# A second tile for the natural layout of x, and an earlier load of the third block, in a convolution and feed-forward kernel

## The chip, the cores and the metric

The kernel runs on one core of a Trainium2 chip. The metric is the device time of that core in microseconds, lower being better. The engines are named as the profile names them: PE for the matrix engine (PEld for its weight loads), DVE for the vector engine, ACT for the scalar engine, POOL for the general purpose engine, and SP for the engine that only issues transfers. "SPq" and "POOLq" in a profile line stand for the queue of such an engine. Each engine takes its instructions in the order in which they were put into its queue, and waits at an instruction until the semaphores that it names have been counted up.

## The reference

```python
x:      (8, 4096, 192) float32      weight: (8, 7) float32
w_in:   (192, 2048) float32         w_out:  (2048, 192) float32

w = softmax(weight, axis=-1)                       # 8 heads of 24 channels, 7 taps
y[b, s, c] = sum_k w[head(c), k] * x[b, s - 6 + k, c]   # causal, zeros before s = 0
x2 = y.reshape(32768, 192)
h  = x2 @ w_in
out = (h * sigmoid(h)) @ w_out                     # (32768, 192) float32
```

A short causal convolution over the sequence, with one set of seven taps for each head, is followed by a feed-forward layer with a SiLU.

## The kernel before

The 32768 tokens are worked through in 32 blocks of 1024 tokens (two halves of 512). A block passes through these stages, each with its function:

- `load` (line 132): twelve transfers on SP, issued on line 140, of 64 KB each, bring the block's x into the tile `nat`. There is one such tile. It has 128 partitions (32 tokens or channels for each of four groups) and three slices, one for each `k`, so four transfers belong to each slice.
- `turn_in` (line 422): DVE transposes one slice of `nat` into `xt` (line 425), so that channels lie on the partitions.
- `halo_in` (line 437): the six columns of `xt` ahead of each half are filled. For the first half POOL copies them from a small tile `tail` (line 442), which was saved from the block before. For the second half SP issues a transfer from the end of the first half (line 443). Then the end of this block is saved for the next (`tail_of`, line 435, a transfer on SP).
- `conv` (line 446): seven taps for each slice. From the third block on, the first tap is a multiplication on DVE (line 454) and the other six are multiply-adds on DVE (line 457). They read `xt` with its six extra columns and write their result back into `nat`, over the x that was there.
- `spread` (line 464): SP copies a finished slice of `nat` into the tile `dup` (line 474), in an arrangement that PE can use.
- `win` (line 478): DVE forms sums and differences of `dup` (lines 491 and 494).
- `product` and `plain` (lines 579 and 591): the first matrix product on PE. ACT copies partial results out of PSUM (line 615), DVE adds them up (line 611, `X`, `a` and `b` in the plan), and ACT applies the SiLU (lines 627 and 632).
- `sum_g` and `out_slot` (lines 635 and 653): differences of the results on DVE, and the second matrix product on PE (line 683).
- `merge`, `turn_out`, `store_out`: the results are combined on DVE and ACT, transposed on DVE (line 764) and stored by SP (line 772).

Both products use a scheme with fewer multiplications than a plain one, which needs sums and differences of the weights. Blocks 1 to 31 take this form. While the first block runs in a plain form (`up_plain`, `down_plain`, lines 529 and 702), DVE converts the float64 weights (`round_in`, `round_out`, all recorded on line 123) and POOL forms the sums of weights (`combine` and `combine_out`, recorded on line 319). A few 192 KB transfers that POOL issues itself (line 307, `ws<-wr`) supply POOL with swapped halves of the weights.

The order of the work is written out by hand in the string `PLAN`. Its slots are separated by bars, and each holds tokens: `i.1` is `turn_in` of slice 1 of the next block, `ha.0` its `halo_in`, `v.10` tap 0 of slice 1 of the next block's convolution, `sp.2` its `spread` of slice 2, `ld.1` a load of slice 1, `X2.0` one of the additions on line 611. A leading `-` means the block before, and `+` the block after. The plan is run once per block, for block numbers 1 to 33, after a separate piece of code for the first block. `step` leaves out whatever is in the set `did`. Instructions made by the wrappers `vec`, `act`, `pool` or `pin` keep the order in which the program gives them. The others, among them the transfers of `load` for any block but the first, are placed by a scheduler.

Because `nat` holds x first and the convolution's result later, the x of the next block can be loaded into a slice only when `spread` has copied that slice's result away. In the plan, `ld.0` comes at the end of a block (`+ld.0`) and `ld.1` and `ld.2` near the start of the next.

Around the end of the first block the program gives, in this order: the convolution of the second block, which is still going on beside `down_plain`, its three spreads, its `win` steps, three transposes and twelve stores of the first block's output, `+ld.0` for the third block, and then the plan for block 1, in which the DVE runs `i.1`, `i.2`, `i.0`, then `v.10`, `v.00`, `v.01`, `v.02`, `v.11`, `v.12` for the third block, and then `X2.0`.

Of the kernel before, what the change touches and what calls it, by code (L numbers as in the profile page):

```python
# [9 lines left out]
F32 = mybir.dt.float32  # L10
# [7 lines left out]
def kernel(  # L18
# [31 lines left out]
    P = 128  # L50
    R = 64
    NK = D // R
    grp = D // H
    pad = K - 1
    TB = 512
# [5 lines left out]
    SQ = 32  # L61
# [8 lines left out]
    xpool = ctx.enter_context(tc.tile_pool(name="xp", bufs=1))  # L70
# [44 lines left out]
    def pin(ins):  # L115
        return tc.keep_in_program_order(ins)
# [13 lines left out]
    nats, xts, gs = {}, {}, {}  # L130

    def load(b, ks=range(NK)):
        if b not in nats:
            nats[b] = nats[0] if b else xpool.tile([P, NK, TB // SQ, SQ], F32, tag="nat", name="nat")
        nat = nats[b]
        for k in ks:
            for i in range(P // SQ):
                c = R * k + SQ * (i % 2)
                queue = nc.scalar if not b and k == 0 and i % 2 == 0 else nc.sync
                ins = queue.dma_start(  # L140
                    out=nat[SQ * i : SQ * i + SQ, k, :, :],
                    in_=x_v[2 * b + i // 2][:, :, c : c + SQ],
                )
                if not b:
                    pin(ins)
# [32 lines left out]
    for k in range(NK):  # L178
        rows_k = hot[SQ * k : SQ * k + SQ]
        for sign, base in ((1, 0), (-1, grp - 1)):  # L180
# [5 lines left out]
                base=base + sign * R * k,  # L186
# [4 lines left out]
    for e in range(2):  # L191
# [6 lines left out]
            base=0,  # L198
# [166 lines left out]
    def combine_out(j):  # L365


        def a_(u, a):
            return wo[j][:, a, :, HD * u : HD * u + HD]

        x_ = [wx[j][:, i, :, :] for i in range(3)]
        comb(x_[0], a_(1, 0), a_(1, 1), ALU.add)
        comb(x_[1], x_[0], a_(0, 0), ALU.subtract)
        comb(x_[2], a_(0, 1), x_[1], ALU.subtract)
        comb(a_(1, 0), a_(0, 0), a_(1, 0), ALU.subtract)
# [191 lines left out]
    def product(b, g, r):  # L567
        e = int(r in ON_B and (g, r) != SWAP)
        if r in RIGHT:
            rhs = rows(wins[b], e)[:, RIGHT[r], :]  # L570
        else:
            rhs = rows(dups[b], e)[:, SLOT[e][X_OF[r]], :]
        if r in (13, 11):
            to, first = banks[XBANK[2 if r == 13 else 4]], False
        else:
            c = next(c for c in range(3) if r in CHAINS[c])
            to, first = chain_bank(g, c), r == CHAINS[c][0]
        pin(
            nc.tensor.matmul(  # L579
                to, raw(g, *LEFT[e][r], e), rhs, start=first, stop=True, skip_group_check=True  # L580
            )
        )

    def plain(b, n, k):
        a, j, own = PLAIN
        first = (b, n) not in begun
        begun.add((b, n))
        for e in range(2) if n else (0,):
            cols = slice(e * TB // 2, (e + 1) * TB // 2) if n else slice(0, TB)
            pin(  # L590
                nc.tensor.matmul(  # L591
                    banks[PLAIN_BANKS[n and 1 + e]][:, cols],
                    rows(wr[j] if own == e else ws[j], e)[:, a, k, :],
                    rows(dups[b], e)[:, SLOT[e][2 * k + n], cols],
                    start=first,
                    stop=True,
                    skip_group_check=True,
                )
            )
# [5 lines left out]
    def sums_h(b, name, g):  # L605

        o = int(name[1:])
        t1, t2, t3 = (chain_bank(g, c) for c in range(3))

        def add(out_, u, v, op=ALU.add):  # L610
            pin(nc.vector.tensor_tensor(out_, u, v, op=op))  # L611

        if name[0] == "u":
            us[b, g, o] = upool.tile([P, TB], F32, tag="u", name="u")
            pin(nc.scalar.copy(us[b, g, o], t1))  # L615
        elif name[0] == "X":
            add(banks[XBANK[o]], us.pop((b, g, o)), t2)
        elif name[0] == "a":
            add(h_of(b, g, o), us.pop((b, g, o)), t2)
        elif name[0] == "b":  # L620
            c = us.get((b, g, o), None)
            c = h_of(b, g, o) if c is None else c
            add(c, c, t3, ALU.subtract)
        else:
            h = h_of(b, g, o)
            src = {3: t1, 2: banks[XBANK[2]], 4: banks[XBANK[4]]}.get(o, h)
            pin(nc.scalar.activation(h, src, AF.Silu))  # L627

    def silu_plain(b, i):
        cols = slice((i - 1) * TB // 2, i * TB // 2) if i else slice(0, TB)  # L630
        h = h_of(b, None, int(i > 0))[:, cols]
        pin(nc.scalar.activation(h, banks[PLAIN_BANKS[i]][:, cols], AF.Silu))


    def sum_g(b, j, i):

        t = sums.setdefault((b, j), {})
        if i // 2 not in t:
            t[i // 2] = tpool.tile([P, 2, 2 * TB], F32, tag="t", name="t")

        def of(a, n):
            return gs[b, j, a][:, n, :, :].rearrange("p e t -> p (e t)")

        u, v = (
            (lambda: (of(0, 1), of(0, 0))),
            (lambda: (of(1, 1), t[0][:, 0, :])),
            (lambda: (of(1, 1), of(0, 1))),
            (lambda: (of(1, 0), t[0][:, 1, :])),
        )[i]()
        engine = pool if f"t.{j}{i}" in ON_POOL else vec  # L650
        engine.tensor_tensor(t[i // 2][:, i % 2, :], u, v, op=ALU.subtract)
# [106 lines left out]
    def turn_out(b, i):  # L758
        if b not in osbs:
            osbs[b] = tpool.tile([P, 4, TB // SQ, SQ], F32, tag="t", name="osb")  # L760
        osb = osbs[b]
        top = HD if b else P
        pin(
            nc.vector.transpose(
                osb[0:top, i, :, :].rearrange("p k c -> p (k c)"), cmbs[b][0][0:top, i, :]
            )
        )

    def store_out(b, i):
        for q in range((HD if b else P) // SQ):  # L770
            n, c = (i % 2, HD * (i // 2) + SQ * q) if b else (q // 2, R * i + SQ * (q % 2))
            nc.sync.dma_start(  # L772
                out=out_v[2 * b + n][:, :, c : c + SQ], in_=osbs[b][SQ * q : SQ * q + SQ, i, :, :]
            )

    plan = [slot.split() for slot in PLAN.split("|")]
    did, later = set(), []
    closing = f"S3.{QUEUE[-1]}"
    BACK = {"-": 1, "=": 2, "+": -1}
    base = {t.lstrip("-=+") for s in plan for t in s}  # L780
# [9 lines left out]
    def step(b, token):  # L790

        if token[0] in BACK:
            b, token = b - BACK[token[0]], token[1:]
        name, arg = token.split(".") if "." in token else ("", "")
        if b < 0 or b >= NB or not name or (b, token) in did:
            return
        if b == NB - 1 and token in held:
            return
        if b == NB - 1 and token[:3] == "D3." and (b, closing) not in did:
            later.append(token)  # L800
            return
        did.add((b, token))
        digits = [int(c) for c in arg]
        if name[0] == "P":
            product(b, digits[0], int(name[1:]))
        elif name == "L":
            plain(b, *digits)
        elif name == "SL":
            silu_plain(b, *digits)
        elif name[0] in "uXabS":  # L810
            sums_h(b, name, digits[0])
        elif name == "t":
            sum_g(b, *digits)
        elif name[0] == "D":
            i, (j, e) = int(name[1]), digits
            for half in range(2) if i == 3 and b == NB - 1 else (None,):
                out_slot(b, j, i, e, half)
        elif name[0] in "Mzyx":
            merge(b, name, *digits)
        elif name == "o":  # L820
            turn_out(b, *digits)
        elif name == "st":
            store_out(b, *digits)
        elif name == "ld":
            if b + 1 < NB:
                load(b + 1, digits)
        elif b + 1 < NB:
            {"i": turn_in, "ha": halo_in, "v": conv, "sp": spread, "w": win}[name](
                b + 1, *digits[: 1 + (name == "v")]
            )  # L830
        if (b, token) == (1, "ha.0"):
            assert not any(t[0] == "D" for c, t in did if c == 1)
            for j in range(NJ):
                combine_out(j)
        if b == NB - 1 and token == closing:
            for t in later:
                step(b, t)
# [152 lines left out]
    for g in (0, 1, 4, 2, 3):  # L990
        for e in range(2):
            combine(g, e)
    step(0, "sp.0")
    beside = FIRST.split("|")
    for _, s in zip_longest(down_plain(0), beside, fillvalue=""):
        for t in s.split():
# [2 lines left out]
        turn_out(0, k)  # L999
        store_out(0, k)  # L1000
    did.update((0, t) for t in base if t[0] not in "ivw")
    for t in (t for s in plan for t in s if t[0] == "+"):
        step(0, t)

    banks = [bank() for _ in range(8)]
    begun = set()
# [36 lines left out]
```

## Time and profile before

| What | Value |
|---|---|
| Median of three runs | 2418.29 us (2417.76 to 2418.6) |
| The profiled execution: its own time, and its span | 2419.24 us, 2417.5 us |
| PE busy | 2389.8 us, 99% of the span |
| DVE busy | 2138.2 us, 88% |
| ACT busy | 1147.8 us, 47% |
| POOL busy | 114.1 us, 5%; 18.22 us of the 20 us from 100 to 120 us |
| DMA | 106.54 MB, a mean of 44 GB/s |
| `nat<-in_x_dram` on SP | 382 issues of 64 KB, median 2.4 us to landing |

The profile describes one execution. Its time of 2419.24 us is 1.74 us more than its span, and 0.95 us more than the median of the three timed runs. Busy shares are averages over the whole span, and say little about a stage of 20 us, so the stages have to be looked at one by one. The entry "idle before, releaser" of a row says how long an engine stood still ahead of an instruction, and what ended that. Where an instruction waits for several semaphores, only the last of them is named.

### The profile page before, as it was taken

How to read it: one execution, taken by the hardware profiler on the slowest of the kernel's cores; microseconds unless marked ns; L12 is line 12 of the kernel's file. 1: busy time of each engine (PE TensorE's matmuls, PEld its weight loads, DVE VectorE, ACT ScalarE, POOL GpSimd, SP SyncE). 2: the span in 40 equal slices, each digit the busy share in tenths (PEclk: the TensorE clock that was granted, in tenths of full speed). 3: DMA queues.
4: the chain of work that ended last, by engine and by line, in shares of the span. 5: the costliest groups of instructions: out<-in, count | busy, mean ns of one | idle time of the engine just before them, and what ended most of it. 6: DMA issues, size and time to landing. Idle time of an engine off the chain costs nothing.

```text
span 2417.5 us, 43655 instructions
## 1 busy us (share of the span) xinstructions
PE 2389.8 (99%) x17630; PEld 981.6 (41%) x17630; DVE 2138.2 (88%) x2967; ACT 1147.8 (47%) x2183; POOL 114.1 (5%) x169
## 2 busy tenths in 40 slices
PE   9799999999999999999999999999999999999998
PEld 5234433444433444434444334443344443344433
DVE  8789888999889898889998899988899988999876
ACT  4145444455444554444554445544445544455443
POOL 5800000000000000000000000000000000000000
PEclk9999999999999999999999999999999999999999
DMA  6311222221222212222212222122222122221111
GB/s 146 70 38 24 42 45 45 51 43 27 47 41 48 51 24 44 43 44 51 45 27 45 41 48 51 26 41 46 42 51 48 24 44 42 48 51 33 34 33 17
DMA packets 451242, 106.54 MB, mean 44 GB/s; under 512 B 423584, under 2 KB 428704, under 8 KB 451040
## 3 DMA queue, kind: packets, MB, share of 16 engines
q1 hardware_dynamic: 447392, 101.78, 23.0%
q8 instruction: 138, 2.26, 0.4%
q0 software_dynamic: 448, 1.58, 0.3%
q10 hardware_dynamic: 3200, 0.39, 0.1%
q14 instruction: 64, 0.52, 0.1%
HBM read 31.46 MB, written 25.17 MB: 23 GB/s over the span
## 4 chain that ended last, share of the span: by engine, by line
PE 94%; DVE 3%; SPq 1%; issue 1%; DMA 1%; ACT 0%; DVEq 0%; ACTq 0%
PE ps L683 47%; PE ps L579 45%; PE ps L591 2%; DVE two L123 1%; DVE nat L457 1%; DVE mh L123 0%; DMA nat<-in_x_dram 0%; SPq L140 0%; SPq L772 0%; DMA dup<-nat 0%; DVE t L123 0%; SPq L474 0%; DVE wo L123 0%; DVE xt L425 0%; DMA xt<-xt 0%
## 5 line engine op out<-in xcount | busy, mean ns | idle before, releaser
L579 PE MATMUL ps<-win,ws 64*128 64x512 f32 x1550 | 704.1, 610 | 17.9 <-DVE ps L611 17.2
L683 PE MATMUL ps<-g,wo 128*32 128x512 f32 x2976 | 708.7, 594 | 0.0
L579 PE MATMUL ps<-win,wr 64*128 64x512 f32 x1550 | 656.5, 609 | 1.1 <-DVE win L491 1.1
L615 ACT COPY u<-ps 128x512 f32<-128x512 f32 x775 | 450.4, 586 | 211.0 <-PE ps L579 196.6
L683 PE MATMUL ps<-t,wo 128*32 128x512 f32 (+2 forms) x4528 | 543.6, 446 | 0.0
L683 PE MATMUL ps<-t,wx 128*32 128x512 f32 x2976 | 491.7, 594 | 0.1
L627 ACT ACTIVATE g<-g 128x512 f32<-128x512 f32 x465 | 279.1, 628 | 438.9 <-DVE g L611 438.9
L457 DVE SCALAR_TENSOR_TENSOR nat<-xt,taps,nat 128x512 f32<-128x512 f32 x564 | 419.8, 749 | 7.7 <-ACT nat L452 3.7
L579 PE MATMUL ps<-dup,wr 64*128 64x512 f32 x868 | 411.8, 594 | 0.0
L123 DVE TENSOR_TENSOR t<-g 128x1024 f32<-128x1024 f32 x248 | 302.0, 1218 | 54.1 <-PE ps L683 53.2
L579 PE MATMUL ps<-dup,ws 64*128 64x512 f32 x682 | 345.7, 603 | 0.0
L123 DVE TENSOR_TENSOR t<-g,t 128x1024 f32<-128x1024 f32 x248 | 302.7, 1221 | 45.9 <-PE ps L683 44.8
L579 PEld LDWEIGHTS ps<-win,wr 64*128 64x128 f32 x1550 | 234.5, 186 | 235.5 <-issue 87.4
L611 DVE TENSOR_TENSOR g<-u,ps 128x512 f32<-128x512 f32 x465 | 314.3, 681 | 15.0 <-PE ps L579 14.1
L579 PEld LDWEIGHTS ps<-win,ws 64*128 64x128 f32 x1550 | 240.4, 186 | 177.7 <-DVE ps L611 68.8
L627 ACT ACTIVATE g<-ps 128x512 f32<-128x512 f32 x465 | 263.6, 596 | 56.5 <-PE ps L579 56.5
L683 PEld LDWEIGHTS ps<-t,wo 128*32 128x32 f32 x4528 | 179.2, 110 | 239.3 <-issue 228.6
L611 DVE TENSOR_TENSOR ps<-u,ps 128x512 f32<-128x512 f32 x310 | 214.2, 691 | 58.9 <-ACT u L615 26.0
L683 PE MATMUL ps<-g,wx 128*32 128x512 f32 x1488 | 246.8, 595 | 0.0
L683 PEld LDWEIGHTS ps<-t,wx 128*32 128x32 f32 x2976 | 115.5, 110 | 269.4 <-issue 267.9
L683 PEld LDWEIGHTS ps<-g,wo 128*32 128x32 f32 x2976 | 162.0, 110 | 135.4 <-issue 135.4
L742 ACT COPY cmb<-ps 96x512 f32<-96x512 f32 x30 | 17.4, 581 | 418.8 <-PE ps L683 418.8
(89 smaller groups left out, 1830.6 us busy)
## 6 DMA issues: line engine op xcount, KB each, us to landing
dup<-nat SPq DMA_DIRECT2D x345, 128.0 KB, 2.3
nat<-in_x_dram SPq DMA_DIRECT2D x382, 64.0 KB, 2.4
out_dram<-osb SPq DMA_DIRECT2D x376, 64.0 KB, 2.0
raw<-in_moe_w_out_dram SPq DMA_DIRECT2D x8, 384.0 KB, 3.4
raw<-in_moe_w_in_dram SPq DMA_DIRECT2D x12, 192.0 KB, 5.0
ws<-wr POOLq DMA_DIRECT2D x8, 192.0 KB, 3.8
raw<-in_moe_w_in_dram SPq DMA_DIRECT2D x6, 128.0 KB, 3.1
xt<-xt SPq DMA_DIRECT2D x31, 4.5 KB, 1.9
```

Source lines behind the costliest of these rows:

```text
L123: return lambda *args, **kw: pin(getattr(self.engine, name)(*args, **kw))
L457: nc.vector.scalar_tensor_tensor(out=dst, in0=src, scalar=tap, in1=dst, op0=ALU.mult, op1=ALU.add)
L579: nc.tensor.matmul(to, raw(g, *LEFT[e][r], e), rhs, start=first, stop=True, skip_group_check=True)
L591: nc.tensor.matmul(banks[PLAIN_BANKS[n and 1 + e]][:, cols], rows(wr[j] if own == e else ws[j], e)[:, a, k, :], rows(dups[b], e)[:, SLOT[e ...
L611: pin(nc.vector.tensor_tensor(out_, u, v, op=op))
L615: pin(nc.scalar.copy(us[b, g, o], t1))
L627: pin(nc.scalar.activation(h, src, AF.Silu))
L683: nc.tensor.matmul(accs[b][at][SQ * q : SQ * q + SQ, to], lhs[:, e, SQ * k : SQ * k + SQ], rhs[:, e, ts(q, TB // 4) if i == 5 else to], st ...
L742: pin(nc.scalar.copy(c[0], acc[0][0:n, :]))
```

## The change

```diff
     def load(b, ks=range(NK)):
         if b not in nats:
-            nats[b] = nats[0] if b else xpool.tile([P, NK, TB // SQ, SQ], F32, tag="nat", name="nat")
+            nats[b] = nats[b % 2] if b > 1 else xpool.tile([P, NK, TB // SQ, SQ], F32, tag="nat", name="nat", bufs=2)
         nat = nats[b]
...
     step(0, "sp.0")
+    load(2)
     beside = FIRST.split("|")
     for _, s in zip_longest(down_plain(0), beside, fillvalue=""):
...
     did.update((0, t) for t in base if t[0] not in "ivw")
-    for t in (t for s in plan for t in s if t[0] == "+"):
-        step(0, t)
+    did.update((1, t) for t in base if t[:2] == "ld")
```

There are now two `nat` tiles, and blocks use them in turn: even blocks the first, odd blocks the second. The whole x of the third block (number 2) is loaded in the program ahead of `down_plain` of the first block, and no longer by `+ld.0` after the first block and by `ld.1` and `ld.2` in the plan of block 1. Those two tokens are entered in `did` for block 1, so that they are left out there. All later loads stay at their tokens. No computation is changed, and the number of loads is the same. The second tile takes 6 KB more in each partition.

The built instruction lists of the two kernels, set side by side, have the same instructions in the same order on PE, DVE, ACT and POOL. Only SP's list differs. There the twelve new loads lie among the transfers of the output weights (line 242): two issues of line 242, then three loads, then two more of line 242, then nine loads. Twelve loads of the next odd block (number 3) take the places that the loads of the third block had among the first spreads and stores, and of these the last three, which stood ahead of lines 443 and 435, now stand behind them:

```
before: ... stores (772) x12 | loads (140) x3 | halo (443) | tail (435) | spread (474) ...
after:  ... stores (772) x12 | halo (443) | tail (435) | loads (140) x3 | spread (474) ...
```

From there on the two lists show the same repeating pattern, with the loads running one block further ahead in the new one.

## The prediction

> **What bounds the kernel now.** I read the page first, to see which engine fills the span.
>
> ```profile
> span 2417.5 us, 43655 instructions
> PE 2389.8 (99%) x17630; PEld 981.6 (41%) x17630; DVE 2138.2 (88%) x2967; ACT 1147.8 (47%) x2183; POOL 114.1 (5%) x169
> ```
>
> PE leaves 2417.5 - 2389.8 = 27.7 us idle. Next I asked for two whole blocks as windows of 76 us; the columns are length, then busy time of PE, PEld, DVE, ACT and POOL, the clock, DMA share and GB/s.
>
> ```profile
> 208.00:284.00 76.00, 76.00 (x564) 31.09 (x562) 68.23 (x96) 37.02 (x72) 0.11 (x1) 1.00 0.23 41
> 1000.00:1076.00 76.00, 76.00 (x576) 30.78 (x572) 68.74 (x95) 35.82 (x68) 1.07 (x1) 1.00 0.23 41
> ```
>
> PE is busy for the whole of both, while DVE is idle for 7 to 8 us. The waits of PE between 130 and 2380 us come back empty, and among those of DVE there is none for a transfer. A load that arrives earlier can gain nothing in these blocks, as x is never late there. So I asked for all waits of PE and DVE, for those that lie outside.
>
> ```profile
> PE ps L579 <- DVE ps L611: 17.2, 1, 17.2
> PE ps L579 <- DVE win L491: 1.1, 1, 1.1
> ...
> DVE xt L425 <- DMA nat<-in_x_dram: 9.5, 2, 8.3
> ...
> DVE nat L454 <- DMA xt<-xt: 2.1, 1, 2.1
> ```
>
> The columns are the total, the number of waits and the longest. One stall of 17.2 us makes up most of PE's idle time. It has to do with x: DVE waits 8.3 us once for a load of nat. The timeline from 106 to 127 us shows who is last; its columns are start, length, engine and line.
>
> ```profile
> 107.69 6.35 SPq L772 DMA_DIRECT2D out_dram<-osb  x12
> 108.78 0.66 DVE L425 STREAM_TRANSPOSE xt<-nat 128x512 f32<-128x512 f32 x1
> ...
> 114.08 1.58 SPq L140 DMA_DIRECT2D nat<-in_x_dram  x3
> ...
> 117.73 1.31 DVE L425 STREAM_TRANSPOSE xt<-nat 128x512 f32<-128x512 f32 x2 [8.29 <-DMA nat<-in_x_dram]
> ...
> 119.09 0.64 SPq L443 DMA_DIRECT2D xt<-xt  x1
> 119.46 1.14 POOL L319 TENSOR_TENSOR wo<-wo 128x192 f32<-128x192 f32 x2
> ...
> 120.54 0.19 POOL L442 COPY xt<-tail 64x18 f32<-64x18 f32 x1
> ...
> 121.10 0.88 DVE L454 TENSOR_SCALAR nat<-xt,taps 128x512 f32<-128x512 f32 x2 [2.07 <-DMA xt<-xt]
> 122.02 2.99 DVE L457 SCALAR_TENSOR_TENSOR nat<-xt,taps,nat 128x512 f32<-128x512 f32 x4
> 124.92 0.69 DVE L611 TENSOR_TENSOR ps<-u,ps 128x512 f32<-128x512 f32 x1
> ...
> 125.67 1.22 PE L579 MATMUL ps<-win,ws 64*128 64x512 f32 x1 [17.22 <-DVE ps L611]
> ```
>
> Read upwards from PE: it waits for X2.0 on line 611, which stands in DVE's queue behind four taps, two first taps (line 454) and the transposes. The transposes wait for three loads which stand in SP's queue behind twelve stores. The halo transfer (line 443) waits for the transposes. That is the chain the profile names. The reader should also see the POOL row at 120.54: the copy into the halo's other half. POOL worked through weight sums without a gap up to it, and the copy ended at 120.73, only 0.37 us before the first tap began. A wait for several semaphores names its last one only, and this first tap needs POOL's copy too.
>
> **What the Trainium skill says.** "Perfetto Trace Analysis", section "Identifying the Most-Contended Engine": improve the busiest engine, though a matmul's busy time is no measure of the distance from its peak. Here I use PE's idle gaps, not its busy share, and the trace agrees that only the start and the end have any. "DMA: Bandwidth & Descriptors", section "Issuing engines are not separate DMA queues": transfers issued by any engine share the same 16 DMA engines. So the new loads could slow POOL's own transfers; no row of before shows such a meeting. "SBUF — State Buffer", section "Who interferes with whom": a VectorE instruction with two SBUF inputs contends with a GpSimd one that reads SBUF. The trace agrees in kind: 64x128 sums on line 319 take 0.45 us each from 109 to 115 us, with DVE nearly idle, and 0.79 us at 92 to 99 us beside DVE's taps.
>
> **The change, part by part.**
>
> *The removed wait.* Loads of block 2 no longer come last. Its x is in by about 72 us (worked out below), well before 108.78. The second and third transposes follow the first at 108.78 + 0.66 = 109.44 and end at 109.44 + 1.31 = 110.75 instead of 119.04. That is 8.29 us earlier.
>
> *The halo transfer.* SP is done with the stores at 107.69 + 6.35 = 114.04. Line 443 now stands right behind them, so it is issued at about 114.08 instead of 119.09. The old one landed at 120.97 (the chain of waits gives it 1.88 us), so the new one lands at 114.08 + 1.88 = 115.96, 5.01 us earlier.
>
> *What is late next.* The first tap waits for DVE, for this transfer and for POOL. POOL's list has not changed, and its copy stands behind all but one of the weight sums, as before. None of these waits for x. POOL is busy for 18.22 of the 20 us from 100 to 120, and from 108 to 120.54 its rows follow each other with gaps below 0.1 us. So the copy ends at 120.73 again. In before DVE began 121.10 - 120.97 = 0.13 us after the landing; with the same delay after POOL it begins at 120.86. The gain is 121.10 - 120.86 = 0.24 us. Its bounds are 0 (if POOL's true end is later than its row, as POOL's rows are rough) and 0.37 us (if DVE could start at the instant at which the row ends). I take 0.24. The later chain (0.88, 2.99 and 0.69 us of DVE, then PE at 125.67) moves with it unchanged: PE's stall becomes 17.0 us.
>
> *Transposes moved beside POOL.* Two of 0.66 us each now lie at 109.4 instead of 117.7, beside POOL either way. A sum cost 0.45 us at 107.32 and 107.84 beside the output transposes and 0.45 us later beside nothing, so they cost POOL nothing. The other bound is a delay of all their length, 1.3 us.
>
> *The twelve new loads.* All are issued by SP, behind the second last pair of line 242, which starts at 53.83. The first three use 3 x 0.67 us (seven loads at 38.74 took 4.69 us, so 0.67 each) while SP would stand waiting for DVE to free the buffer of the last pair. That pair ends at 53.83 + 9.78 = 63.61. The other nine follow and take 9 x 0.67 = 6.0 us, to 69.6; with 2.4 us to landing they are in at 72.0. SP has nothing else until line 443 at 80.04, so 10 us of its idle time cover them. DVE reads the last weight pair at 71.21; it lands 63.61 + 3.4 = 67.0, which leaves 4.2 us. POOL's transfer `ws<-wr` is issued from 72.28, and POOL waits 2.50 us for it (74.27 to 76.77); the loads are in 0.3 us before it starts. Cost: nothing, cover 0.3 us. Without that cover POOL, which now sets the end of the stall, would be late by what is left to drain, one for one. Nine loads carry 9 x 64 = 576 KB; at 158 GB/s, the mean of the first 20 us, that is 3.6 us, which I take as the far bound.
>
> *The wait on SP at line 435.* It waits for POOL (0.3 us before) and will now be reached at 114.7. It may stand there until POOL's copy, 120.7. Behind it are three loads of block 3 and the spreads that before issue at 153.78. Nobody needs these within 30 us: nothing.
>
> *The blocks after.* Loads of later blocks still wait for the spread that frees their tile (SP waits 106.2 us for this in all, 59 times, before), now one block further ahead. SP has hundreds of us of waits for stores and spreads to cover this, and no engine waited for x. Gain and loss nil. At the end the last load comes a block sooner; the chain there is PE, then merges and stores.
>
> The sum against the profiled execution: 2419.24 - 0.24 = 2419.0. The timed median lies 0.95 us below that execution, so I carry the difference over: 2418.29 - 0.24 = 2418.05, or 2418.0.
>
> **Rivals.**
>
> *The stall shrinks by the full 5 us.* If POOL's copy were not in the way, the first tap would start at 115.96 + 0.13 = 116.09, and PE 5.01 us sooner: 2413.3. For it speaks the profile's naming of x and the halo transfer as releasers. Against it stand POOL's wait in the built list and its gapless rows to 120.54. Chance 0.04.
>
> *POOL becomes late, and the kernel slower.* Place: 72.28 us, where POOL's transfer meets the nine loads. It decides once the last load lands after 72.3, by a load issue above 0.70 us or a pair of line 242 that is issued later than 62.6. With the far bound it gives 2418.3 + 3.6 - 0.2 = 2421.7. To exceed 0.2% POOL would have to be late by 4.84 + 0.24 = 5.1 us, which needs loads that land in the 5.4 us of the slowest one seen and DVE late for its weights as well. For it: the cover is 0.3 us, and POOL now sets the pace. Against it: the DMA windows show 0.22 and 0.26 of the engines busy at 60 to 70 us. Chance 0.12, of which 0.05 beyond 0.2%.
>
> *It does nothing at all.* If loads of block 2 are put so that DVE still waits for one, the time is 2418.3. The built list speaks against it; chance 0.04, and it can't be told from the forecast.
>
> **How the numbers follow.** The forecast has the other 0.80. About 0.2% (4.8 us) is what a measurement of this kernel can tell from no change. The forecast, the idle rival and 0.07 of the slower one lie within it, and of the 0.04 of the first rival 0.03 lies just beyond: faster 0.03, slower 0.05, same 0.92. The range takes 2418.05 less 0.13 for the other bound of the gain and 1.7 us for the spread of runs (twice the 0.84 us of the three before), so 2416.2; upwards 1.3 us for the transposes and most of the middle of the slower rival, so 2420.5.
>
> **What would show it right or wrong.** Right: transposes of line 425 without a gap at 108.8 to 110.8; line 443 near 114.1; a wait of some 10 us of the first tap on line 454, now put down to POOL's line 442; POOL's copy again at about 120.5; PE's stall at 17.0 us; PE without idle time after 130. Wrong: the copy earlier than 118 or the stall below 13 us (the first rival); a wait of POOL for `ws<-wr` well above 2.5 us, or the copy after 122 (the second); any idle time of PE in a window of a later block.

## The result and the profile after

The changed kernel took 2420.26 us in the median of four runs (2418.74 to 2420.99), the kernel before beside it 2418.44 us. The ratio is 1.0007, with a 95% interval of 0.999 to 1.0025: no change that can be measured. When both were timed again, in the first experiment below, the ratio came out as 0.9997 (0.9989 to 1.0005), with 2418.67 us against 2419.8 us. In that larger set, 43 executions of the kernel before lie between 2417.21 and 2421.36 us, so a single run can be 2 us off either way.

The profiled execution took 2420.68 us, with a span of 2418.9 us. The first two lines of PE's waits, in the columns total, number and longest:

```profile
PE ps L579 <- DVE ps L611: 17.8, 1, 17.8
PE ps L579 <- POOL wr L319: 1.3, 1, 1.3
```

Among DVE's waits, in the same columns, one is new:

```profile
DVE nat L454 <- POOL xt L442: 13.7, 1, 13.7
```

The wait of 8.3 us for a load of `nat` has gone, and PE's stall is still there, if anything longer. The timeline from 104 to 130 us shows what DVE waits for instead:

```profile
106.23 6.34 SPq L772 DMA_DIRECT2D out_dram<-osb  x12
...
107.33 1.85 DVE L425 STREAM_TRANSPOSE xt<-nat 128x512 f32<-128x512 f32 x3
...
112.68 0.63 SPq L443 DMA_DIRECT2D xt<-xt  x1
113.41 0.62 SPq L435 DMA_DIRECT2D tail<-xt  x1
...
121.58 1.13 POOL L319 TENSOR_TENSOR wo<-wo 128x192 f32<-128x192 f32 x2
122.66 0.19 POOL L442 COPY xt<-tail 64x18 f32<-64x18 f32 x1
...
122.89 1.19 DVE L454 TENSOR_SCALAR nat<-xt,taps 128x512 f32<-128x512 f32 x2 [13.71 <-POOL xt L442]
124.11 2.99 DVE L457 SCALAR_TENSOR_TENSOR nat<-xt,taps,nat 128x512 f32<-128x512 f32 x4
127.02 0.69 DVE L611 TENSOR_TENSOR ps<-u,ps 128x512 f32<-128x512 f32 x1
...
127.76 1.22 PE L579 MATMUL ps<-win,ws 64*128 64x512 f32 x1 [17.82 <-DVE ps L611]
```

The three transposes now follow each other without a gap, and the halo transfer stands right behind the stores. Both were to be seen if the load was really out of the way. But the first tap starts 0.04 us after POOL's copy ends (122.66 + 0.19 = 122.85), and 8.3 us after the halo transfer must have landed (112.68 + 1.88 = 114.56). The wait moved from a transfer to a small copy behind POOL's weight sums, which in the kernel before ended 0.37 us ahead of the tap.

In this execution that copy came 2.12 us later than in the profile of before, although DVE was earlier (transposes at 107.33 instead of 108.78). Where POOL fell behind is read from its timeline in the two kernels. Before:

```profile
28.69 0.49 POOL L319 TENSOR_TENSOR ws<-ws 64x128 f32<-64x128 f32 x1 [3.94 <-DMA ws<-wr]
29.73 0.67 POOL L319 TENSOR_TENSOR ws<-ws 64x128 f32<-64x128 f32 x1 [0.55 <-DMA ws<-wr]
...
31.09 3.37 POOL L319 TENSOR_TENSOR ws<-ws 64x128 f32<-64x128 f32 x4
```

POOL's timeline in the changed kernel, over the same instructions, with the first two sums from narrower windows that keep them apart:

```profile
29.02 3.35 POOL L319 TENSOR_TENSOR ws<-ws 64x128 f32<-64x128 f32 x1 [4.76 <-DMA ws<-wr]
...
32.45 1.06 POOL L319 TENSOR_TENSOR ws<-ws 64x128 f32<-64x128 f32 x1
...
34.60 3.37 POOL L319 TENSOR_TENSOR ws<-ws 64x128 f32<-64x128 f32 x4
```

The same four sums start 3.5 us later. Only 0.33 us of this was there at the first sum (29.02 against 28.69), which waits for POOL's own transfer. That first sum stands in the trace with 3.35 us, against 0.49 in before, and so the second starts 2.7 us later. What held it is not shown. The first of the new loads is issued on SP at 52.67 us, 18 us after the four sums began, so the loads can't be the cause. What follows the stall took as long as before: PE has no wait between 131 and 2380 us, and from the end of the stall to the end of the span there are 2418.9 - 127.76 = 2291.1 us here and 2417.5 - 125.67 = 2291.8 us in before.

### The profile page after: what moved, and what is told of

Read it like the earlier page. It is cut to its first block, busy times and chain, and to the rows that moved or that the text cites. A ratio compares the mean times of both kernels' runs of the same rounds, so it can differ in the third digit from the quotient of the medians.

```text
span 2418.9 us, 43592 instructions
## 1 busy us (share of the span) xinstructions
PE 2389.8 (99%) x17630; PEld 981.6 (41%) x17630; DVE 2137.2 (88%) x2967; ACT 1149.1 (48%) x2183; POOL 116.6 (5%) x169
## 4 chain that ended last, share of the span: by engine, by line
PE 94%; DVE 0%; ACT 0%; issue 0%; POOL 0%; ACTq 0%
PE ps L683 47%; PE ps L579 45%; PE ps L591 2%; DVE t L123 0%; DVE nat L457 0%; DVE cmb L123 0%; ACT u L123 0%; DVE g L611 0%; DVE nat L454 0%; DVE osb L123 0%; DVE ps L611 0%; DVE u L611 0%; ACT u L615 0%; POOL wo L319 0%; ACTq L871 0%
## 5 line engine op out<-in xcount | busy, mean ns | idle before, releaser
L579 PE MATMUL ps<-win,ws 64*128 64x512 f32 x1550 | 703.7, 610 | 18.5 <-DVE ps L611 17.8
```

Of the source, the lines that this page charges most:

```text
L579: nc.tensor.matmul(to, raw(g, *LEFT[e][r], e), rhs, start=first, stop=True, skip_group_check=True)
```

## The experiments

Each was compared with runs of the kernel before on the same chip, and a ratio is to those (it need not be the quotient of the two medians). Theory A is that POOL's copy sets the start of the tap; theory B, that the second tile moved other tiles in memory and that this costs time; theory C, that the first 1.8 us were chance.

**The changed kernel once more** (no edit).

> The changed kernel once more. Theory A (POOL's halo copy sets the start of the third block's first tap, and POOL's pace through the weight sums differs from run to run): PE's stall ends 5.1 us after the copy wherever that lies, the copy lies anywhere from 120 to 123 us, and the times spread over 2 us around 2420. Theory B (the second tile has moved other tiles in memory, and that costs time each time): again 2420.3, with a ratio of 1.0008 and little spread. Theory C (the 1.8 us are chance): the ratio goes back to 0.9999.

It took 2418.67 us (2416.37 to 2421.09), ratio 0.9997 (0.9989 to 1.0005). In its profile the copy lay at 122.57 us and PE went on at 127.67, 5.1 us later, as in the other profile. The same 5.1 us lie between the two in the next kernel (120.33 and 125.43) and in the one with the load made twice (124.69 and 129.78). The 1.8 us were chance (C), and a spread of over 4 us is what A expects where POOL's pace differs from run to run. The placement of the tiles is the same here as in the first set, so a ratio below 1 speaks against B; the next kernel tests B alone.

**Room for two tiles, one used.** No instruction differs from the kernel before, only the places of the tiles.

```diff
-nats[b] = nats[0] if b else xpool.tile([...], F32, tag="nat", name="nat")
+nats[b] = nats[0] if b else xpool.tile([...], F32, tag="nat", name="nat", bufs=2)
```

> The kernel before with room for two nat tiles of which it uses one, so that every tile lies where it lies in the changed kernel, and no instruction differs. Theory A: as before, 2418.4, or late by as much as POOL's copy happens to be later than 120.7. Theory B: 2420.3, as in the changed kernel. Theory C: 2418.4.

It took 2420.11 us (2416.92 to 2422.46), ratio 1.0003 (0.9995 to 1.0011). The 2420.11 looks like the 2420.3 of B, but the kernel before, timed beside it, lay at 2419.8 and not at the 2418.4 of the first set. So the placement has no cost that can be measured; the interval leaves room for 0.11%, or 2.7 us. Its profile, of an execution of 2417.49 us, adds something on the kernel before. The timeline around the stall:

```profile
117.11 1.30 DVE L425 STREAM_TRANSPOSE xt<-nat 128x512 f32<-128x512 f32 x2 [8.40 <-DMA nat<-in_x_dram]
...
118.48 0.64 SPq L443 DMA_DIRECT2D xt<-xt  x1
...
120.33 0.19 POOL L442 COPY xt<-tail 64x18 f32<-64x18 f32 x1
...
120.56 1.19 DVE L454 TENSOR_SCALAR nat<-xt,taps 128x512 f32<-128x512 f32 x2 [2.14 <-POOL xt L442]
```

With the same instructions as before, the last releaser here is POOL's copy. The loads and POOL are so close together that now one and now the other comes last.

**The halo copy of the third block on ACT**, in the changed kernel and in the kernel before. ACT makes it at about 102 us; POOL loses this one instruction.

```diff
-            nc.gpsimd.tensor_copy(xt[0:R, :, 0:pad], tails.pop(b))
+            (act.copy if b == 2 else nc.gpsimd.tensor_copy)(xt[0:R, :, 0:pad], tails.pop(b))
```

In the changed kernel:

> The changed kernel with the third block's halo copy on ACT instead of POOL, the one copy alone. Theory A: the first tap no longer waits for POOL but for the halo transfer, which landed at 114.6 us in the trace of the changed kernel (issued 112.68, 1.9 us to landing); it starts at 114.7 instead of 122.9, PE's stall falls from 17.8 to about 10 us, and the time by 6 to 8 us, to 2412 to 2414. Theory B: 2420.3, as the tiles lie where they lay. If the loads of x bound after all: no gain.

It took 2414.49 us (2413.13 to 2415.54), ratio 0.998 (0.9972 to 0.9988), 4.2 us less than the changed kernel beside it. From its timeline:

```profile
108.45 1.85 DVE L425 STREAM_TRANSPOSE xt<-nat 128x512 f32<-128x512 f32 x3
...
113.81 0.63 SPq L443 DMA_DIRECT2D xt<-xt  x1
...
115.80 1.85 DVE L454 TENSOR_SCALAR nat<-xt,taps 128x512 f32<-128x512 f32 x2 [5.50 <-DMA xt<-xt]
...
117.69 3.94 DVE L457 SCALAR_TENSOR_TENSOR nat<-xt,taps,nat 128x512 f32<-128x512 f32 x4
...
121.55 0.68 DVE L611 TENSOR_TENSOR ps<-u,ps 128x512 f32<-128x512 f32 x1
...
122.29 1.22 PE L579 MATMUL ps<-win,ws 64*128 64x512 f32 x1 [12.65 <-DVE ps L611]
```

The tap waits for the halo transfer and starts 7.09 us sooner than in the changed kernel's profile (115.80 against 122.89). A holds. PE goes on only 5.47 us sooner, because the first taps now run beside POOL's sums: the pair on line 454 took 1.85 us instead of 1.19, the four on line 457 3.94 instead of 2.99, together 1.61 us more.

The whole span is 2418.9 - 2411.8 = 7.1 us shorter, so a further 1.6 us lie behind the stall. Windows of the changed kernel show what differs there; the columns are those of the prediction, with the granted clock third from the end:

```profile
127.76:130.00 2.24, 2.24 (x6) 1.18 (x8) 1.48 (x3) 0.09 (x1) 0.00 (x0) 0.50 0.00 0
130.00:133.00 3.00, 3.00 (x14) 2.04 (x12) 0.95 (x2) 0.88 (x2) 0.00 (x0) 0.50 0.02 5
134.00:137.00 3.00, 3.00 (x16) 1.23 (x15) 2.07 (x4) 2.16 (x4) 0.00 (x0) 1.00 0.01 3
```

The same with the copy on ACT:

```profile
122.29:125.00 2.71, 2.71 (x8) 1.52 (x10) 2.24 (x3) 0.56 (x1) 0.34 (x1) 0.50 0.02 6
126.00:130.00 4.00, 4.00 (x22) 1.84 (x20) 1.89 (x4) 2.55 (x5) 0.00 (x0) 1.00 0.00 0
```

When PE goes on, it first works at half the clock, for about 6 us in the changed kernel and about 3 us here (the windows from 133 to 134 us there and from 125 to 126 us here lie across the rise, with means of 0.65 and 0.75). My estimate from these figures is that half of such a time is lost, 3 us against 1.5, which is near the 1.6 us; it was not tested by itself. So the two profiled executions, 2420.68 and 2413.47 us, differ by 7.2 us, within the 6 to 8 us expected. The medians differ by only 4.2 us: the expectation started from that profiled execution of the changed kernel, which is 2 us slower than its later median of 2418.67 us.

In the kernel before:

> The kernel before with the same copy on ACT. Theory A: the loads of nat behind the twelve stores still come last, the first tap starts at about 121 us as before, and the time is 2418.0 to 2418.5. If POOL alone bound the kernel before: a gain like that of the changed kernel with the copy on ACT, 5 us or more. Theory B: 2418.4.

It took 2418.74 us (2417.46 to 2419.85), ratio 0.9998 (0.9989 to 1.0006). The transposes waited 8.5 us for `nat`, the tap started at 120.22 us behind the halo transfer, and PE stalled 16.5 us. Without the second tile, taking POOL out of the way gains nothing that can be measured; its 13 times spread over 2.4 us, the 43 of the kernel before over 4.2 us.

**The copy made 25 times on POOL**, in the changed kernel. The same small copy is repeated, into the same place.

```diff
-            nc.gpsimd.tensor_copy(xt[0:R, :, 0:pad], tails.pop(b))
+            [nc.gpsimd.tensor_copy(xt[0:R, :, 0:pad], tails[b]) for _ in range(25 if b == 2 else 1)]
```

> The changed kernel with the third block's halo copy on POOL made 25 times in place of once (the same small copy each time). Theory A (POOL's copy sets the start of the first tap): the last copy ends 24 times 0.15 to 0.19 us later, so PE's stall ends 3.6 to 4.6 us later and the time rises by as much, to 2422 to 2424. If the copy does not bind: unchanged, near 2419.

It took 2426.1 us (2423.66 to 2428.07), ratio 1.0024 (1.0015 to 1.0032). The timeline:

```profile
123.73 6.27 POOL L442 COPY xt<-tail 64x18 f32<-64x18 f32 x25
...
130.04 1.20 DVE L454 TENSOR_SCALAR nat<-xt,taps 128x512 f32<-128x512 f32 x2 [20.73 <-POOL xt L442]
```

The copies follow each other every 0.25 us, (6.27 - 0.19) / 24, and not every 0.15 to 0.19 us as I had assumed, so they added 6.1 us. The time is 2426.1 - 2419.82 = 6.3 us above that of the kernel before beside it, and 7.4 us above the 2418.67 of the changed kernel in the first experiment, where single runs lie up to 2 us off. What is added to POOL here reaches the end of the kernel, as A says.

**The load made twice**, in the changed kernel, so that 21 loads stand ahead of the second block's halo transfer.

```diff
-    load(2)
+    load(2), load(2)
```

> The changed kernel with the load of the third block's x made twice, into the same tile, so that 21 loads stand in place of nine ahead of the second block's halo and run until about 76 us. If the loads can slow POOL's own transfer at 72 to 76 us (the slower rival of the prediction): POOL waits longer for it than the 2.1 to 2.5 us seen, its copy comes later by the same, and the time is 2421 to 2423. If they can't: 2418.7, as the changed kernel, and POOL's wait stays where it was.

It took 2418.92 us (2417.21 to 2421.56), ratio 0.9997 (0.9989 to 1.0005), like the changed kernel. SP issued the loads from 60.54 to 72.70 us, and POOL, whose transfer was issued at 77.90 in this execution, waited 2.13 us for it. The copy was at 124.69 us there, but POOL was late before the nine loads, which are 21 here, began: its first sum started at 30.3 us, against 28.7 in before, and one sum that took 0.77 us in the changed kernel stands with 4.01 us from 53.61 on. It lies beside the first three new loads, issued from 53.17; these are in the changed kernel too (from 52.67), with no such sum beside them, and the cause stays open. The prediction's slower rival is not seen at this number of loads: they cost nothing that can be measured. Its meeting of loads and POOL's transfer did not take place in this execution, though, since the last load must have landed near 75 us (72.70 and a median of 2.4), before that transfer was issued.

**The halo transfer on ACT too**, in the changed kernel with the copy on ACT.

```diff
-        nc.sync.dma_start(out=xt[R:P, :, 0:pad], in_=xt[0:R, :, TB : TB + pad])
+        (nc.scalar if b == 2 else nc.sync).dma_start(out=xt[R:P, :, 0:pad], in_=xt[0:R, :, TB : TB + pad])
```

> The changed kernel with the copy on ACT, and the third block's halo transfer issued by ACT, so that it no longer stands behind the twelve stores on SP. Theory A (with POOL out of the way the transfer is the last to come): it is issued at about 110.3 us, right after the third transpose, instead of 113.8, and lands 3.4 us sooner; the first tap starts near 112.5 and the time falls from 2414.5 to about 2411. Rival (the taps now run beside POOL's weight sums, which last until 122 us, and are slowed by them): the tap starts as early, but each tap takes longer and the gain is 2 us or less.

It took 2410.4 us (2410.04 to 2410.91), ratio 0.9958 (0.9945 to 0.997): the fastest of all. From its timeline:

```profile
109.79 0.70 ACTq L443 DMA_DIRECT2D xt<-xt  x1
...
110.53 0.58 ACT L615 COPY u<-ps 128x512 f32<-128x512 f32 x1 [8.13 <-DVE xt L425]
...
111.17 1.22 PE L579 MATMUL ps<-win,wr 64*128 64x512 f32 x1 [8.45 <-DMA out_dram<-osb]
...
112.36 1.11 DVE L454 TENSOR_SCALAR nat<-xt,taps 128x512 f32<-128x512 f32 x2 [2.61 <-DMA xt<-xt]
```

The transfer no longer waits for the stores, and the tap starts 3.4 us sooner. PE has a new wait, though: ACT's copies of partial results (line 615) now stand behind that transfer, which waits for the transposes. The row for PE names a store as the releaser, but PE went on 0.06 us after ACT's copy ended at 111.11, which itself had stood behind the issue. The name in such a row is an inference, and here it probably misleads: in the kernel with one tile and both moves, below, PE's wait at this place is put down to ACT's line 615.

**X2.0 ahead of the taps**, in the changed kernel with the copy on ACT, alone and with the halo transfer on ACT. In block 1 the tokens for transposes, halo and taps wait in a list until X2.0 has run, and are then taken one to a slot.

```diff
-    begun = set()
+    begun, fifo = set(), []
...
             for t in s:
-                step(b, t)
+                if b == 1 and t[0] in "ihv" and (fifo or (1, "X2.0") not in did):
+                    fifo.append(t)
+                else:
+                    step(b, t)
+            if fifo and (1, "X2.0") in did:
+                step(1, fifo.pop(0))
...
```

> The changed kernel with the copy on ACT, and in block 1 the transposes, the halo and the taps for the third block put behind X2.0 on DVE, one token to a slot of the plan. Theory D (PE stalls because X2.0 stands behind the transposes and taps in DVE's queue, whoever makes these late): X2.0 runs at 109 us, PE goes on at once, and its next wait is for the addition that now stands behind the taps, at about 120; the stall of 12.6 us splits or shrinks and the time falls by 1 to 4 us from 2414.5. Rival: DVE loses in the stages after what PE gains here, and the time is 2414.5 or more.

Alone it took 2413.8 us (2412.4 to 2414.11), ratio 0.9971 (0.9961 to 0.9982). PE went on early, and then waited 6.2 us for a later addition, which DVE had behind the taps, until 122.04 us, and 2.3 us for another, until 126.42. Without this edit the stall ended at 122.29. The stall is split, and the end gains little; a difference of 0.7 us from 2414.49 is within the intervals.

> Both of the last two together. If each works on its own part of the stall: below 2411, perhaps 2408 to 2410, the fastest of all. If they are the same microseconds: as the better of the two.

Together they took 2411.37 us (2410.86 to 2412.2), ratio 0.9962 (0.9949 to 0.9976), no better than the halo transfer alone. So the place of X2.0 in DVE's queue is not worth more than about a microsecond. In their trace PE goes on early and then waits twice for additions that DVE makes after taps, 1.72 us until 118.60 and 3.72 us until 123.82; with the halo transfer alone its last wait of over a microsecond ended at 111.17.

**Both moves to ACT with one tile**, in the kernel before (both of the edits on lines 442 and 443).

> The kernel before, with one nat tile, and with both moves of the fastest kernel (halo copy and halo transfer of the third block on ACT). If the second tile is needed for the gain: the transposes still wait for the loads behind the twelve stores (116.9 us), the halo transfer follows at about 118, the tap at 120.2 as before, and the time is 2418 to 2419. If the two moves alone carry the gain: near 2410.4.

It took 2418.11 us (2416.7 to 2419.3), ratio 0.9993 (0.9985 to 1.0001). The transposes waited 8.21 us for `nat` and ended at 117.96; the tap started at 120.29. The second tile, with the earlier load, is worth about 7.7 us (2418.11 - 2410.4, with the kernel before beside them at 2419.94 and 2419.82) once the copy and the transfer are off POOL and SP, and nothing measurable while they are on them.

## Why the prediction was right

- **The removed wait**: right. The transposes followed each other at 107.33, and none waited for x.
- **The halo transfer**: right. It stood behind the stores and landed 8 us before it was needed.
- **What is late next**: right, and the point on which the result hangs. DVE waited for POOL's line 442. The gain named there, 0.24 us with bounds of 0 and 0.37, can't be told from nothing; the tap followed POOL's copy after 0.04 us and not 0.13. The step "the copy ends at 120.73 again" failed in its number: it ended at 122.85 in the profile, and at other times elsewhere. PE's stall was 17.8 us and not 17.0. In the prediction's own list a copy after 122 us is a sign of the slower rival, POOL made late by the loads. The copy did come after 122, but POOL had fallen behind before any new load was issued.
- **The twelve new loads**: right that they cost nothing that can be measured. The cover I gave as 0.3 us was larger: the nine loads took 5.31 us and not 6.0, from 61.53 us on, and POOL's transfer came at 75.72. Even 21 loads had no cost that can be measured. One reading was wrong: that no row of before shows POOL's transfers slowed beside others. The two issued from 23.47 us, with SP's loads at 23.84 beside them and the DMA engines busy throughout (a share of 0.99 from 26 to 30 us), took a median of 5.3 us to land, and the two from 35.55, where the share was 0.33, took 2.9 us.
- **The wait on SP at line 435**: it did not stand until POOL's copy, as I held possible; it was issued at 113.41, and nothing hung on it.
- **The blocks after**: right. PE is busy for the whole of both windows.

```profile
208.00:284.00 76.00, 76.00 (x565) 31.10 (x563) 68.74 (x97) 37.59 (x72) 0.11 (x1) 1.00 0.24 43
1000.00:1076.00 76.00, 76.00 (x584) 30.99 (x580) 68.36 (x96) 35.84 (x68) 1.07 (x1) 1.00 0.23 41
```

- **The spread of runs** was sized too small. I took 1.7 us from three runs; 43 runs lie over 4.15 us. The range of 2416.2 to 2420.5 held the median of 2420.26 only just, and with a spread of 4 us that was luck; the later median of 2418.67 lies near the forecast of 2418.05. The term that was missing is POOL's pace: the copy was at 120.3 to 124.7 us in the profiles of kernels in which POOL made it once. Where it comes last the time goes with it: 2417.49 us with the copy at 120.33, 2420.25 at 122.57, 2420.68 at 122.66 and 2421.56 at 124.69.

Of the rivals, most of the full gain of 5 us appeared as soon as the copy was taken from POOL: PE went on at 122.29 instead of 125.67, 3.4 us sooner than in before. The rest went to the taps' slower run beside POOL: from the first tap to PE it was 122.29 - 115.80 = 6.5 us, instead of 125.67 - 121.10 = 4.6 us in before. The reading that POOL stood in its way is therefore shown, not only argued. Why POOL falls behind in some executions was not settled. It does so before any new load: the four sums that start at 31.09 us in before start at 32.92 in the kernel with one tile and both moves, and anywhere from 30.77 to 34.75 in the kernels with two tiles. The latest of these all have two tiles, but with one profile of each kernel that is too few to blame the tile; the timed runs show no cost of it.

## What to carry to other kernels

A wait for several semaphores shows only the last of them, so before taking it away, list what else the instruction waits for and when each of these came: here a copy of 0.19 us had ended 0.37 us before the tap began, and left at most that much of an 8 us wait to be gained. Small copies that the main path needs don't belong behind a long queue of side work on the same engine. A second buffer, which was worth nothing by itself, became worth 7.7 us when the two things behind it were moved as well.

## What the runs showed of the hardware that was not expected

- DVE's taps ran slower beside POOL's sums: a pair of first taps 1.85 us instead of 0.88 in the profile of before, and four multiply-adds 3.94 instead of 2.99. In the other kernels with the copy on ACT the pair took 1.08 to 1.22 us, and four multiply-adds, where they stand in one row, 3.41 to 3.74. An operation that starts earlier isn't always worth all of its lead.
- PE's granted clock was 0.50 around the stall and stayed there after PE went on: until after 131 us in before, where the stall ended at 125.67, and until after 133 us in the changed kernel, where it ended at 127.76. From 140 to 2400 us it was 1.00 in both.
- POOL's own 192 KB transfers landed in 2.7 to 5.5 us in the profile of before and in 2.7 to 7.0 us in that of the changed kernel, and its longest wait for one was 3.9 and 4.8 us. Both of these waits lie before 30 us, where the two programs issue the same.
- POOL's copies of 64x18 elements took 0.19 us each by their rows, but came every 0.25 us.
